# A transformer block with adaptive norms: group 3's V products summed on VectorE instead of TensorE, group 0's second norm in two parts

## The chip, the core and the metric

The kernel runs on one core of a Trainium2 chip. The metric is the device time of one execution in microseconds (us). TensorE is called PE here, VectorE DVE, ScalarE ACT, GpSimd POOL and SyncE, which issues nearly all DMAs, SP, as the profile calls them.

## What is computed

```python
# x: 2048 rows of 512;  sa, ca, ga, sb, cb, gb = six parts of silu(c) @ w_mod
h = layernorm(x) * (1 + ca) + sa
q, k, v = h @ wqkv                                  # 32 heads of 16
logits[h, s, w] = q[h, s] . k[h, s - 2*w] / 4       # w = 0..7; s - 2*w < 0 is masked
attn = softmax(logits over w)
o[h, s] = sum over w of attn[h, s, w] * v[h, s - 2*w]
x = x + ga * (o @ wo)
h = layernorm(x) * (1 + cb) + sb
x = x + gb * ((gelu(h @ w_gate) * (h @ w_up)) @ w_down)    # inner width 1792
```

Attention is a window of eight rows at distance two, so it isn't a matrix product over rows: it is eight elementwise products with shifted K, summed over a head's 16 columns, and eight with shifted V, summed over the shifts.

## The kernel before

The 2048 rows are worked in four groups (0 to 3) of 512. For each group: a first norm; its transposition; 12 products for q, k, v (`qkv`, L621; group 0 in halves, L560); logits; softmax; V products; the product with wo (`x1_mm`, L821) added to x (`x1_ev`, L830); a second norm (`norm`, `ln2`); its transposition (`transp`, `transp_ev`, L475, L481, L513) to h; 14 pairs of products g and u (`ffn_mm`, L851); gelu of g to `gl` and a copy of u to `ub` on ACT (L883, L890); their product `hht` on DVE (L901); and eight half products y with w_down (L863), which DVE adds to x as `ot` (L908) and SP stores.

All engines run from one list, `ORDER`: each number names a thread (one generator per kind of work and group), and takes the next instruction from it. Each engine works its instructions strictly in that order and waits in place. Nothing is planned at run time.

**The V path of a group.** Softmax leaves probabilities `e` with rows of a block of 128 by head: partition 32·g + head for row block g, and eight shifts by 128 rows along the free axis. SP stores `e` to memory and loads it back as `PT`, where the partitions are pairs of shift and head (`pt_dma`, L762, L769). V is stored and loaded back four times, shifted, as `V` (`vload`, L659, L667). DVE multiplies both for each j of four (`pv`, L781, 4096 elements each), PE sums over the shifts by a matrix of ones `M` in tiles of 32 columns (`pv_mm`, L800, eight matmuls for each j), and ACT copies the sums to `oT` (`pv_ev`, L811), the left operand of `x1_mm`.

**Buffers.** PSUM has the pools `mm` (4 banks: qkv, g, u, y), `att` (2) and `lg` (1). `gl` and `ub` have three buffers each; a copy into one waits until DVE has made the `hht` of three pairs before. `pv` and `pq` share four buffers called `prod`.

**Group 0's second norm.** Two of its four row blocks are summed on ACT, two on DVE; then comes one reciprocal root for all four on POOL (L452, a `pow`), then four `xn` on DVE (L461). Sixteen transposes on PE (`BY_PE` names it) put them into two PSUM tiles, from which ACT makes h.

Of the kernel before, what the change touches and what calls it, by code (L numbers as in the profile page):

```python
# [106 lines left out]
def kernel(  # L107
# [395 lines left out]
    def transp_ev(key, dkey, dtag, sc, bi, ev, dep):  # L503
        pe = ev in BY_PE
        for dtp in range(2):
            for dd in range(2):
                dt = 2 * dtp + dd

                def f(dt=dt, dtp=dtp, dd=dd):
                    if pe and dt == 0:  # L510
# [2 lines left out]
                    nc.scalar.activation(out=o, in_=B[key, dtp][:, :, dd, :] if pe else o, func=ACT.Identity,  # L513
                                         scale=sc(dt), bias=bi(dt))
# [474 lines left out]
```

## Time and profile before

| what | us |
|---|---|
| median of 3 runs | 236.57 (236.39 to 236.57) |
| the profiled execution | 236.67 |
| its span, first to last instruction | 234.7 |
| PE busy, share of the span | 230.0, 98% |
| DVE busy | 168.8, 72% |
| ACT busy | 150.3, 64% |

A group row of the profile reads: line, engine, operation, what is written from what, shapes, count | busy us in all, mean ns of one | idle time of the engine just before them, and what ended it. A row of the timeline reads: start, duration, engine, line, operation, operands, count. In the chain of work that ended last, each row is a start, a duration and what ran. A DMA row ends with the median us from issue to landing. The 40 slices are of 5.9 us each; a digit is the busy share in tenths. Matmuls are pipelined, and in the groups one of 512 columns shows some 380 ns; in a row of them each adds 216.

### The profile page before, as it was taken

The numbers are of one execution on the slowest core, as the hardware profiler recorded it, in microseconds if no ns is written. First come the engines' busy times: TensorE is split into PE (matmuls) and PEld (weight loads), VectorE is DVE, ScalarE is ACT, GpSimd is POOL, SyncE is SP. The second block draws the span as 40 slices with busy tenths as digits, with TensorE's granted clock in tenths as the row PEclk, the third lists the DMA queues.
The fourth block names the chain that finished last, engine by engine and source line by source line (L and its number), as shares of the span: only waits on it lengthen the run. The fifth ranks groups of instructions, "written<-read, shape, count | busy, mean of one in ns | idle before, by whom it ended". The sixth has DMA issues, their size and how long they took to land.

```text
span 234.7 us, 3714 instructions
## 1 busy us (share of the span) xinstructions
PE 230.0 (98%) x1408; PEld 110.8 (47%) x1408; DVE 168.8 (72%) x242; ACT 150.3 (64%) x281; POOL 19.7 (8%) x37
## 2 busy tenths in 40 slices
PE   7999999999999999999999999999999999999995
PEld 2788454544544444444443444444444444444443
DVE  4799999999999999999999599968422221222222
ACT  6699998588896566947579732084666703666400
POOL 1412323210200000010000004001000000000000
PEclk9999999999999999999999999999999999999999
DMA  6999696997929518036500790500600011000011
GB/s 218 358 340 299 169 249 231 228 313 258 342 80 300 195 14 307 1 61 170 179 3 1 220 270 14 112 22 0 134 3 1 0 45 47 0 0 0 3 45 45
DMA packets 32441, 30.95 MB, mean 132 GB/s; under 512 B 17064, under 2 KB 28328, under 8 KB 32424
## 3 DMA queue, kind: packets, MB, share of 16 engines
q1 hardware_dynamic: 31888, 30.19, 42.4%
q10 hardware_dynamic: 536, 0.53, 0.6%
q8 instruction: 11, 0.18, 0.3%
q14 instruction: 6, 0.05, 0.1%
HBM read 22.78 MB, written 5.31 MB: 120 GB/s over the span
## 4 chain that ended last, share of the span: by engine, by line
PE 85%; DMA 6%; ACT 6%; SPq 1%; issue 1%; ACTq 0%; DVE 0%
PE g_ps L851 20%; PE u_ps L851 20%; PE y_ps L863 19%; PE qkv_ps L621 10%; DMA wm<-in_w_mod_dram 6%; PE x_ps L821 6%; PE o_ps L800 3%; PE LTp L706 3%; PE y_ps L874 1%; PE qkv_ps L560 1%; ACT h L513 1%; ACT hT L513 1%; ACT kT L639 1%; ACT vT L641 1%; PE hTp L475 1%
## 5 line engine op out<-in xcount | busy, mean ns | idle before, releaser
L851 PE MATMUL g_ps<-h,Wg 128*128 128x512 bf16 x224 | 57.7, 379 | 0.1
L851 PE MATMUL u_ps<-h,Wu 128*128 128x512 bf16 x224 | 57.5, 379 | 0.0
L901 DVE TENSOR_TENSOR hht<-gl,ub 128x512 bf16<-128x512 bf16 x56 | 23.1, 419 | 36.8 <-ACT ub L890 36.8
L883 ACT ACTIVATE gl<-g_ps 128x512 bf16<-128x512 f32 x56 | 33.6, 600 | 24.8 <-PE g_ps L851 22.1
L863 PE MATMUL y_ps<-Wd,hht 128*128 128x512 bf16 x210 | 46.1, 379 | 0.0
L890 ACT CAST ub<-u_ps 128x512 bf16<-128x512 f32 x56 | 32.9, 588 | 17.9 <-PE u_ps L851 17.9
L689 DVE TENSOR_TENSOR pq<-qT,kT 128x4096 bf16<-128x4096 bf16 (+1 forms) x17 | 36.3, 2159 | 0.0
L781 DVE TENSOR_TENSOR pv<-PT,V 128x4096 bf16<-128x4096 bf16 x16 | 36.2, 2287 | 0.0
L851 PEld LDWEIGHTS <-Wg 128*128 128x128 bf16 x224 | 21.6, 98 | 27.3 <-issue 1.9
L851 PEld LDWEIGHTS <-Wu 128*128 128x128 bf16 x224 | 21.7, 98 | 26.8 <-issue 0.8
L621 PE MATMUL qkv_ps<-hT,wqkv 128*128 128x512 bf16 x144 | 32.8, 380 | 0.4 <-ACT hT L513 0.3
L863 PEld LDWEIGHTS <-hht 128*128 128x128 bf16 x210 | 20.5, 98 | 24.9 <-issue 0.4
L621 PEld LDWEIGHTS <-wqkv 128*128 128x128 bf16 x144 | 15.9, 114 | 15.8 <-issue 2.6
L908 DVE TENSOR_TENSOR ot<-y_ps,x 128x512 bf16<-128x512 f32 x15 | 10.2, 684 | 17.6 <-PE y_ps L863 17.6
L452 POOL TENSOR_TENSOR rstd<-rstd,neghalf 128x4 f32<-128x4 f32 (+1 forms) x9 | 10.9, 1211 | 120.4 <-DVE rstd L441 62.7
L811 ACT CAST oT<-o_ps 128x512 bf16<-128x512 f32 x16 | 8.9, 597 | 13.8 <-PE o_ps L800 13.8
L821 PE MATMUL x_ps<-woP,oT 128*128 128x512 bf16 x64 | 15.1, 379 | 0.0
L421 DVE BATCH_NORM_STATS2 st<-x 128x6 f32<-128x512 bf16 x19 | 12.5, 680 | 2.6 <-DMA x<-in_A_x_dram 2.5
L513 ACT ACTIVATE h<-h,modT,scl 128x512 bf16<-128x512 bf16 x12 | 8.8, 806 | 4.8 <-DMA h<-xn 4.8
L560 PE MATMUL qkv_ps<-hT,wqkv 128*128 128x256 bf16 x96 | 11.4, 273 | 0.2
L830 DVE TENSOR_TENSOR x<-x_ps,x 128x512 bf16<-128x512 f32 x16 | 10.9, 686 | 0.6 <-PE x_ps L821 0.5
L560 PEld LDWEIGHTS <-wqkv 128*128 128x128 bf16 x96 | 10.2, 114 | 0.9 <-DMA wqkv<-in_A_wqkv_dram 0.4
(80 smaller groups left out, 193.4 us busy)
## 6 DMA issues: line engine op xcount, KB each, us to landing
V<-vscr SPq DMA_DIRECT2D x16, 526.0 KB, 4.8
vscr<-vT SPq DMA_DIRECT2D x4, 528.0 KB, 3.8
wm<-in_w_mod_dram SPq DMA_DIRECT2D x4, 512.0 KB, 6.9
out_dram<-ot SPq DMA_DIRECT2D x15, 128.0 KB, 1.7
Wg<-in_B_w_gate_dram SPq DMA_DIRECT2D x4, 448.0 KB, 6.0
Wu<-in_B_w_up_dram SPq DMA_DIRECT2D x4, 448.0 KB, 7.1
x<-in_A_x_dram SPq DMA_DIRECT2D x3, 512.0 KB, 5.7
Wd<-in_B_w_down_dram SPq DMA_DIRECT2D x3, 512.0 KB, 6.8
```

What stands on the lines that cost most here:

```text
L421: nc.vector.bn_stats(out=k["st", c4][:], in_=src()[:, c4, :])
L513: nc.scalar.activation(out=o, in_=B[key, dtp][:, :, dd, :] if pe else o, func=ACT.Identity, scale=sc(dt), bias=bi(dt))
L560: nc.tensor.matmul(B["qu", h, blk, u][:, jj, :], lhsT=wqkv[blk][:, dt, 2 * u + jj::4], rhs=B["hT", 0][:, 2 * h:2 * h + 2, dt, :], start=st ...
L621: nc.tensor.matmul(ps[:], lhsT=wqkv[blk][:, dt, j::4], rhs=B["hT", sg][:, :, dt, :], start=(dt == 0), stop=(dt == DT - 1))
L689: nc.vector.tensor_tensor(out=B["pq", sg, j][:, :, c0:c1], in0=_ap(B["qT", sg][:, j, c0:c1], [[0, W], [1, c1 - c0]]), in1=_ap(kT[:, j, sg ...
L781: nc.vector.tensor_tensor(out=t[:], in0=_ap(B["PT", sg][:, 0, :], [[SG, 2], [0, 4], [1, SG]]), in1=_ap(v[:, j, 0, :], [[8, 2], [VR, 4], [1 ...
L821: nc.tensor.matmul(ps[:], lhsT=B["oT", sg][:, j, c4 * P:(c4 + 1) * P], rhs=woP[:, j, :], start=(j == 0), stop=(j == 3))
L851: nc.tensor.matmul(ps[:], lhsT=Wt[:, dt, ft * P:(ft + 1) * P], rhs=B["h2T", sg][:, :, dt, :], start=(dt == 0), stop=(dt == DT - 1))
L863: nc.tensor.matmul(ps[:], lhsT=B["hh", sg, ft][:, c4 * P:(c4 + 1) * P], rhs=B["Wd", ft // 4][:, ft % 4, :], start=(ft == 0), stop=(ft == F ...
L883: nc.scalar.activation(out=gl[:], in_=B["g", sg, ft][:], func=ACT.Gelu_apprx_tanh)
L890: nc.scalar.copy(out=ub[:], in_=B["u", sg, ft][:])
L901: nc.vector.tensor_tensor(out=hh[:], in0=B["gl", sg, ft][:], in1=B["ub", sg, ft][:], op=ALU.mult)
```

## The change

1. *Group 3's V path* (`VS = (3,)`). `e` stays where softmax leaves it; it isn't stored and loaded as `PT`. V is loaded so that its partitions agree with `e` (four loads of 32 partitions, `V3`). DVE multiplies (four times 4096 elements, one for each i of four) and then sums over the eight shifts itself by a `tensor_reduce` to 512 elements in bf16 (`O3`). Since O3 has rows along the free axis by head, and `oT` needs heads' columns on partitions, each quarter goes to memory by four DMAs (rows of 128 bf16) and back by one. PE's 32 matmuls and ACT's four copies for group 3 are gone.
2. *Group 0's V products* are made in two halves of 256 rows, and so are their sums (four times 16 matmuls of 256 columns), the copies, and the second norm (two roots on POOL, for two blocks each). Its transposition goes by two DMA transposes of eight blocks in place of PE, and h is scaled in halves, six on ACT and two on DVE. Its x products use the pool `mm`.
3. *Group 1's `vT`* has its buffer in another pool; `qkv` and `ffn_mm` name all their dependencies; the threads have a new order.

The core of the diff:

```diff
-    29, 29, 29, 2, 29, 29, 3, 29, 1, 45, 0, 1, 17, 18, 29, 29, 29, 17, 37, 37, 39, 39, 2, 2, 39, 39, 39, 4, 39,
+    29, 29, 29, 29, 29, 29, 2, 29, 3, 29, 29, 39, 39, 39, 39, 39, 0, 40, 1, 1, 17, 17, 2, 2, 0, 18, 37, 17, 40,
...
-    BY_PE = ("LN1.1", "LN2.0")
+    BY_PE = ("LN1.1",)
...
+        if sg in VS:
+            for g in range(CPS):
+                def f(g=g):
+                    if g == 0:
+                        B["V3", sg] = T("v4", [P, 4, 4, P + VH], BF16, "V3")
+                    src = bass.AP(vscr[sg].tensor, vscr[sg].offset + g * P, [[4 * n, H], [VR, 16], [1, P + VH]])
+                    nc.sync.dma_start(out=B["V3", sg][H * g:H * g + H].rearrange("p i j s -> p (i j) s"), in_=src)
...
     def pt_dma(sg):
+        if sg in VS:
+            for i in range(4):
+                for g in range(CPS):
+                    def f(i=i, g=g):
+                        d = oscr[sg, i]
+                        nc.sync.dma_start(out=bass.AP(d.tensor, d.offset + g * P, [[SG, H], [H * SG, 4], [1, P]]),
+                                          in_=B["O3", sg][H * g:H * g + H, i])
...
+                    nc.sync.dma_start(out=B["oT", sg][:, i, :], in_=oscr[sg, i][:])
...
     def pv(sg):
+        if sg in VS:
+            for i in range(4):
...
+                    nc.vector.tensor_tensor(out=t[:], in0=_ap(B["e", sg][:], [[0, 4], [P, W], [1, P]]),
+                                            in1=_ap(B["V3", sg][:, i, 0, 2:], [[P + VH, 4], [2, W], [1, P]]), op=ALU.mult)
...
+                        nc.vector.tensor_reduce(out=B["O3", sg][:, i], in_=B["pv", sg, i][:].rearrange("p d w s -> p d s w"),
+                                                axis=AX.X, op=ALU.add)
...
+    def pv_half_mm():
+        for h in range(2):
+            for jp in range(2):
...
+                                nc.tensor.matmul(o_ps[H * i:H * i + H, jj, :], lhsT=M[:], rhs=B["pvh", h, jp][:, jj, t, i, :],
+                                                 start=(jj == 0 and t == 0), stop=(jj == 1 and t == 1), tile_position=(0, H * i))
...
+    def transp_half():
+        for h in range(2):
...
+                nc.sync.dma_start_transpose(out=B["h2T", 0][:, 2 * h:2 * h + 2].rearrange("p c d s -> p (c d) s"),
+                                            in_=B["xn2", 0][:, 2 * h:2 * h + 2, :].rearrange("p c d -> p (c d)"))
```

On DVE, around the end of group 1's second stage and the start of group 2's, the order before was this (xn is group 2's second norm, pv are group 3's last products, ot group 1's results, the last rows group 3's x and the first hht of group 2; `hht` numbered in the text as hht 0, 1, ... of a group):

```order
L461 TENSOR_SCALAR xn<-x,mv,rstd 128x512 x4
L781 TENSOR_TENSOR pv<-PT,V_1851 128x4096 x2
L908 TENSOR_TENSOR ot<-y_ps,x 128x512 x3
L830 TENSOR_TENSOR x<-x_ps,x 128x512
L421 BN_STATS st<-x 128x6
```

And now (O is O3, V_1883 is V3, y_ps of `ot` are group 1's):

```order
L463 TENSOR_SCALAR xn<-x,mv,rstd 128x512 x4
L867 TENSOR_REDUCE O_2078<-pv 128x512
L1035 TENSOR_TENSOR ot<-y_ps,x 128x512
L858 TENSOR_TENSOR pv<-e,V_1883 128x4096
L1035 TENSOR_TENSOR ot<-y_ps,x 128x512 x2
L867 TENSOR_REDUCE O_2078<-pv 128x512
L858 TENSOR_TENSOR pv<-e,V_1883 128x4096
L1028 TENSOR_TENSOR hht<-gl,ub 128x512
L867 TENSOR_REDUCE O_2078<-pv 128x512
L858 TENSOR_TENSOR pv<-e,V_1883 128x4096
L1028 TENSOR_TENSOR hht<-gl,ub 128x512 x2
L867 TENSOR_REDUCE O_2078<-pv 128x512
L1035 TENSOR_TENSOR ot<-y_ps,x 128x512
L1028 TENSOR_TENSOR hht<-gl,ub 128x512 x5
```

The four reductions and three products stand ahead of, and between, the first three hht of group 2, and the last ot of group 1 stands behind the fourth reduction. On PE the x products of group 3 moved from behind group 1's last y and the first g of group 2 to behind g 9 of group 2.

On SP's queue the same stretch before held stores and two transposes:

```order
L932 DMA out_dram<-ot 128x512
L481 DMA_TRANSPOSE h_2096<-xn 128x16x128
L932 DMA out_dram<-ot 128x512
L481 DMA_TRANSPOSE h_2226<-xn 128x16x128
L932 DMA out_dram<-ot 128x512 x9
```

Now the sums' stores and loads stand between them:

```order
L483 DMA_TRANSPOSE h_2042<-xn 128x16x128
L1059 DMA out_dram<-ot 128x512
L791 DMA oscr_0_116<-O_2078 32x4x128 x3
L1059 DMA out_dram<-ot 128x512
L791 DMA oscr_0_116<-O_2078 32x4x128
L798 DMA oT<-oscr_0_116 128x512
L791 DMA oscr_1_117<-O_2078 32x4x128 x4
L798 DMA oT<-oscr_1_117 128x512
L791 DMA oscr_2_118<-O_2078 32x4x128 x4
L798 DMA oT<-oscr_2_118 128x512
L791 DMA oscr_3_119<-O_2078 32x4x128 x4
L798 DMA oT<-oscr_3_119 128x512
```

Each quarter of `oT` is loaded behind its four stores; two out stores and group 3's transpose wait behind the last.

Around group 0's second norm DVE had this order before (x is group 0's sum; mx and LTp belong to group 1's softmax):

```order
L830 TENSOR_TENSOR x<-x_ps,x 128x512 x2
L723 TENSOR_REDUCE mx<-LTp 128x128
L830 TENSOR_TENSOR x<-x_ps,x 128x512 x2
L421 BN_STATS st<-x 128x6 x2
L427 BN_AGGR mv<-st 128x2 x2
L441 TENSOR_SCALAR rstd<-mv 128x2
L446 TENSOR_SCALAR rstd<-sums 128x2
L729 TENSOR_TENSOR LTp<-LTp,mx 128x1024
L461 TENSOR_SCALAR xn<-x,sums,rstd 128x512 x2
L461 TENSOR_SCALAR xn<-x,mv,rstd 128x512 x2
```

Now its second half stands so:

```order
L929 TENSOR_TENSOR x<-x_ps,x 128x512 x2
L463 TENSOR_SCALAR xn<-x,sums,rstd 128x512
L423 BN_STATS st<-x 128x6
L463 TENSOR_SCALAR xn<-x,mv,rstd 128x512
L429 BN_AGGR mv<-st 128x2
L443 TENSOR_SCALAR rstd<-mv 128x1
L448 TENSOR_SCALAR rstd<-sums 128x1
L744 TENSOR_REDUCE mx<-LTp 128x128
L463 TENSOR_SCALAR xn<-x,sums,rstd 128x512
L463 TENSOR_SCALAR xn<-x,mv,rstd 128x512
L750 TENSOR_TENSOR LTp<-LTp,mx 128x1024
L710 TENSOR_TENSOR pq<-qT,kT 128x4096
```

The first half's statistic and roots now stand ahead of the last two x sums, and a product of group 2's logits stands between the last xn and the two half h that DVE makes (L956, not shown).

More of the change, by code (lines that the diff above doesn't have):

```diff
@@ L147 @@
     gscr = {b: dram.tile([D], BF16, name=f"gscr{b}") for b in (2, 3, 4, 5)}
+    oscr = {(g, i): dram.tile([P, SG], BF16, name=f"oscr{g}_{i}") for g in (3,) for i in range(4)}
     escr = [dram.tile([P, W, P], BF16, name=f"escr{g}") for g in range(NSG)]
@@ L624, in qkv @@
             tk = [SL["q"]] if (blk, j) == (0, 0) else []
-            yield Op("PE", 0.865, f, after=[f"LN1.{sg}.h{d}" for d in (2, 3)] + [wq0(blk, d) for d in range(DT)], take=[SL["mm"]] + tk,
+            yield Op("PE", 0.865, f, after=[f"LN1.{sg}.h{d}" for d in range(DT)] + [wq0(blk, d) for d in range(DT)], take=[SL["mm"]] + tk,
                      give=[SL["hT"]] if last else [], fire=f"qp.{sg}.{blk}.{j}")
@@ L650, in f @@
                 nc.gpsimd.memset(B["vT", 0][:, :, 0:VH], 0.0)
-        yield Op("POOL", 0.2, f, after=[f"vh.{sg - 1}"] if sg else [], take=[SL["vs"]], fire=f"vz.{sg}")
+        yield Op("POOL", 0.2, f, after=[f"vh.{sg - 1}"] if sg else [], take=[SL["ot4" if sg == 1 else "vs"]], fire=f"vz.{sg}")
     def vload(sg):
@@ L760, in pt_dma, with f @@
     def pt_dma(sg):
+        if sg in VS:
[5 more added lines that the diff above has]
+                                          in_=B["O3", sg][H * g:H * g + H, i])
+                    yield Op("SP", 0.4, f, after=[f"pr.{sg}.{i}"], give=[SL["hT"]] if i == 3 and g == 3 else [], fire=f"os.{sg}.{i}.{g}", lat=0.6)
+                def f(i=i):
+                    if i == 0:
+                        B["oT", sg] = T("ot4", [P, 4, SG], BF16, "oT")
+                    nc.sync.dma_start(out=B["oT", sg][:, i, :], in_=oscr[sg, i][:])
+                yield Op("SP", 0.4, f, after=[f"os.{sg}.{i}.{g}" for g in range(CPS)], take=[SL["ot4"]] if i == 0 else [], fire=f"oT.{sg}.{i}", lat=0.6)
+            return
         def f():
@@ L773, with pv_half, f @@
     smp = {k: pool(k + "_p", 1) for k in ("mx", "e", "ssum", "rinv", "PT")}
-    def pv(sg):
+    def pv_half():
+        for h in range(2):
+            for j in range(4):
+                def f(h=h, j=j):
+                    if j % 2 == 0:
+                        B["pvh", h, j // 2] = T("prod", [P, 2, 2, 4, 256], BF16, "pv")
+                    nc.vector.tensor_tensor(out=B["pvh", h, j // 2][:, j % 2],
+                                            in0=_ap(B["PT", 0][:, 0, 256 * h:], [[SG, 2], [0, 4], [1, 256]]),
+                                            in1=_ap(B["V4", 0][:, j, 0, 256 * h:], [[8, 2], [VR, 4], [1, 256]]), op=ALU.mult)
+                last = h == 1 and j == 3
+                yield Op("DVE", 1.15, f, after=["pt.0.1", f"V4.0.{j}"], take=[SL["prod"]] if j % 2 == 0 else [],
+                         give=[SL["v4"], SL["PT"]] if last else [], fire="pv.0.3" if last else f"pvh.{h}.{j}")
@@ new lines, in pv_half_mm, with f @@
+    def pv_half_mm():
+        for h in range(2):
+            for jp in range(2):
+                def f(h=h, jp=jp):
+                    o_ps = T("att", [P, 2, 256], F32, "o_ps")
+                    B["oh", h, jp] = o_ps
+                    for jj in range(2):
+                        for t in range(2):
+                            for i in range(4):
+                                nc.tensor.matmul(o_ps[H * i:H * i + H, jj, :], lhsT=M[:], rhs=B["pvh", h, jp][:, jj, t, i, :],
+                                                 start=(jj == 0 and t == 0), stop=(jj == 1 and t == 1), tile_position=(0, H * i))
+                yield Op("PE", 0.44, f, quad=True, after=["pv.0.3" if h and jp else f"pvh.{h}.{2 * jp + 1}", "consts"],
+                         take=[SL["att"]], give=[SL["prod"]], fire=f"oh.{h}.{jp}")
@@ new lines, in pv_half_ev, with f @@
+    def pv_half_ev():
+        for h in range(2):
+            for jp in range(2):
+                def f(h=h, jp=jp):
+                    if ("oT", 0) not in B:
+                        B["oT", 0] = T("ot4", [P, 4, SG], BF16, "oT")
+                    nc.scalar.copy(out=B["oT", 0][:, 2 * jp:2 * jp + 2, 256 * h:256 * h + 256], in_=B["oh", h, jp][:])
+                yield Op("ACT", 0.485, f, after=[f"oh.{h}.{jp}"], take=[] if h or jp else [SL["ot4"]], give=[SL["att"]],
+                         fire=f"oTh.{h}.{jp}")
@@ new lines, in pv, with f @@
+    def pv(sg):
+        if sg in VS:
+            for i in range(4):
+                def f(i=i):
+                    t = T("prod", [P, 4, W, P], BF16, "pv")
+                    B["pv", sg, i] = t
+                    nc.vector.tensor_tensor(out=t[:], in0=_ap(B["e", sg][:], [[0, 4], [P, W], [1, P]]),
+                                            in1=_ap(B["V3", sg][:, i, 0, 2:], [[P + VH, 4], [2, W], [1, P]]), op=ALU.mult)
+                yield Op("DVE", 2.2, f, after=[f"p.{sg}"] + [f"V4.{sg}.{g}" for g in range(CPS)], take=[SL["prod"]],
+                         give=[SL["v4"], SL["es"]] if i == 3 else [], fire=f"pv.{sg}.{i}")
+                def f(i=i):
+                    if i == 0:
+                        B["O3", sg] = T("hT", [P, 4, 4, P], BF16, "O3")
+                    with nc.allow_low_precision("the eight terms add up in f32; only the sum is rounded, as it is on its way from PSUM"):
+                        nc.vector.tensor_reduce(out=B["O3", sg][:, i], in_=B["pv", sg, i][:].rearrange("p d w s -> p d s w"),
+                                                axis=AX.X, op=ALU.add)
+                yield Op("DVE", 4.4, f, take=[SL["hT"]] if i == 0 else [], give=[SL["prod"]], fire=f"pr.{sg}.{i}")
+            return
@@ L822, in f @@
                                      start=(j == 0), stop=(j == 3))
-            yield Op("PE", 0.865, f, after=[f"oT.{sg}.3", "woS"], take=[SL["att"]], give=[SL["ot4"]] if c4 == 3 else [],
+            yield Op("PE", 0.865, f, after=([f"oTh.{c4 // 2}.{jp}" for jp in range(2)] if sg == 0 else [f"oT.{sg}.{i}" for i in ((0, 1, 2, 3) if sg in VS else (3,))]) + ["woS"], take=[SL["att" if sg else "mm"]], give=[SL["ot4"]] if c4 == 3 else [],
                      fire=f"x1p.{sg}.{c4}")
@@ new lines, in transp_half, with f @@
+    def transp_half():
+        for h in range(2):
+            def f(h=h):
+                if h == 0:
+                    B["h2T", 0] = T("h2", [P, CPS, DT, P], BF16, "h2")
+                nc.sync.dma_start_transpose(out=B["h2T", 0][:, 2 * h:2 * h + 2].rearrange("p c d s -> p (c d) s"),
+                                            in_=B["xn2", 0][:, 2 * h:2 * h + 2, :].rearrange("p c d -> p (c d)"))
+            yield Op("SP", 0.9, f, after=[f"LN2.0.x{2 * h + 1}"], take=[] if h else [SL["h2"]], give=[SL["xn"]] if h else [],
+                     fire=f"LN2.0.th{h}", lat=0.6)
@@ new lines, with half_ev, f @@
+    HALF_DVE = ((1, 2), (1, 3))
+    def half_ev(eng):
+        for h in range(2):
+            for dt in range(DT):
+                if ((h, dt) in HALF_DVE) != eng:
+                    continue
+                def f(h=h, dt=dt):
+                    o = B["h2T", 0][:, 2 * h:2 * h + 2, dt, :]
+                    if eng:
+                        nc.vector.tensor_scalar(out=o, in0=o, scalar1=scl[:, 4 + dt:5 + dt], scalar2=modT[:, 4 + dt:5 + dt],
+                                                op0=ALU.mult, op1=ALU.add)
+                    else:
+                        nc.scalar.activation(out=o, in_=o, func=ACT.Identity, scale=scl[:, 4 + dt:5 + dt],
+                                             bias=modT[:, 4 + dt:5 + dt])
+                yield Op("DVE" if eng else "ACT", 0.25 if eng else 0.5, f, after=[f"LN2.0.th{h}", "mod3", "mod4"],
+                         fire=f"LN2.0.h{dt}.{h}")
@@ L956 @@
     pl.spawn(exp_table())
+    for sg in range(1, NSG):
+        pl.spawn(ln1_ev(sg, True))
+    for sg in range(NSG):
+        pl.spawn(ln2_ev(sg, True) if sg else half_ev(True))
+    pl.spawn(ln2(0, 2, 4))
+    pl.spawn(norm_act(lambda: B["x", 0], lambda c4: [f"x1.0.{c4}"], "LN2.0", 2))
     with tc.manual_schedule():
```

58 lines of the change are left out of this document (37 added, 21 removed), and 71 rows, old and new, of the table ORDER.

## The prediction

> **What bounds the kernel now.** I read the page's engine shares and slices first, then the waits of the matmul engine, then the chain in order of time.
>
> ```profile
> span 234.7 us, 3714 instructions
> PE 230.0 (98%) x1408; PEld 110.8 (47%) x1408; DVE 168.8 (72%) x242; ACT 150.3 (64%) x281; POOL 19.7 (8%) x37
> ...
> PE   7999999999999999999999999999999999999995
> ...
> DVE  4799999999999999999999599968422221222222
> ```
>
> TensorE (PE) is busy in 38 of 40 slices to nine tenths or more, so it is the bound from one end to the other. VectorE (DVE) is as full until slice 27 (about 160 us) and nearly idle after it. Work that leaves PE is therefore worth its time, and work that arrives on DVE is free only where DVE's answers still come before PE asks for them.
>
> ```profile
> PE warm_ps L204 <- DVE gB L199: 1.2, 1, 1.2
> PE qkv_ps L621 <- ACT hT L513: 0.3, 1, 0.3
> PE gR_ps L370 <- DMA wm<-in_w_mod_dram: 0.2, 1, 0.2
> ```
>
> PE's whole list of waits is 1.7 us: there is almost no waiting left to remove, so a gain can come only from PE work taken out, and a loss only from a new wait. The chain shows the places that the change touches:
>
> ```profile
> 19.09 1.00 PE hTp L475 x16
> ...
> 57.84 5.18 PE qkv_ps L621 x24
> 64.38 2.14 ACT h L513 x3
> ...
> 141.84 10.58 PE y_ps L863 x49
> 152.41 1.84 PE o_ps L800 x32
> 154.25 1.62 PE y_ps L863 x7
> ...
> 160.35 0.86 PE u_ps L851 x4
> ...
> 183.66 12.09 PE y_ps L863 x56
> ```
>
> The 32 products of group 3's V path stand inside group 1's last products and cost 1.84 us. One product of the second stage (four matmuls, g or u) costs 0.86, a group's eight down products 12.09, a set of sixteen transposes on PE 1.00.
>
> **What the change costs, part by part.**
>
> *Group 3's V products.* PE loses the 32 o_ps matmuls: −1.84. The copies of o_ps on ScalarE go too; ScalarE waited there anyway, so I count nothing for them. DVE keeps four products of 4096 elements and gets four reductions from 4096 to 512 elements, bf16 in SBUF. The trace has no such reduction; these rows bound it:
>
> ```profile
> L781 DVE TENSOR_TENSOR pv<-PT,V 128x4096 bf16<-128x4096 bf16 x16 | 36.2, 2287 | 0.0
> ...
> L901 DVE TENSOR_TENSOR hht<-gl,ub 128x512 bf16<-128x512 bf16 x56 | 23.1, 419 | 36.8 <-ACT ub L890 36.8
> ...
> L421 DVE BATCH_NORM_STATS2 st<-x 128x6 f32<-128x512 bf16 x19 | 12.5, 680 | 2.6 <-DMA x<-in_A_x_dram 2.5
> ...
> L908 DVE TENSOR_TENSOR ot<-y_ps,x 128x512 bf16<-128x512 f32 x15 | 10.2, 684 | 17.6 <-PE y_ps L863 17.6
> ...
> L723 DVE TENSOR_REDUCE mx<-LTp 128x128 f32<-128x1024 f32 x4 | 4.9, 1218 | 0.0
> ...
> L689 DVE TENSOR_TENSOR pq<-qT,kT 128x2048 bf16<-128x2048 bf16 x2 | 2.4, 1212 | 0.0
> ```
>
> The bf16 product takes 1212 ns for 2048 elements and 2287 for 4096, so 1075 per 2048 and 137 fixed. A reduction of 1024 f32 elements takes 1218, so 1081 per 1024 behind the same 137: half the product's rate. The low end for the new reduction is the product's 2.29 us, the high end 4 × 1081 + 137 = 4.46 us. I take the high end: it is the same operation, and the one row that folds bf16 from SBUF, the statistics over 512 elements, takes 680 ns, as long as a sum with an f32 operand in PSUM (684) and not the 419 of a bf16 product.
>
> The Trainium skill ("VectorE: DVE Perf Modes", section on the perf-mode tier table) says that tensor_reduce has a program for one element per cycle alone, in bf16 as in f32, in SBUF as in PSUM. It agrees with the f32 row's 1218 ns; no run here shows it for bf16. By that rule the sum is the one below; by the rate of the bf16 product row it would be the 234.6 of the first rival.
>
> Now the place. What counts is what stands behind the reductions on DVE. These rows set the clock of that stretch:
>
> ```profile
> 138.03 1.28 DVE L830 TENSOR_TENSOR x<-x_ps,x 128x512 bf16<-128x512 f32 x2
> ...
> 143.79 2.98 POOL L452 TENSOR_TENSOR rstd<-rstd,neghalf 128x4 f32<-128x4 f32 x1 [42.55 <-DVE rstd L441]
> ...
> 146.81 1.38 DVE L461 TENSOR_SCALAR xn<-x,mv,rstd 128x512 bf16<-128x512 bf16 x4 [0.30 <-POOL rstd L452]
> 148.10 4.49 DVE L781 TENSOR_TENSOR pv<-PT,V 128x4096 bf16<-128x4096 bf16 x2
> ...
> 162.84 1.11 POOL L452 TENSOR_TENSOR rstd<-rstd,neghalf 128x4 f32<-128x4 f32 x1 [16.07 <-DVE rstd L441]
> ```
>
> Two products in a row take 4.49 where one takes 2.29: the next instruction starts 0.08 before the last ends. So the steps are 2.20 for a product, 4.38 for a reduction, 0.60 for an ot or a statistic, 0.34 for an hht. I count from Y, the start of group 1's down products (141.84 before). The x sums end at 139.31, Y − 2.5. Then on DVE: two statistics and an aggregate 1.3, the first product 2.2, aggregates 0.3, three hht 1.0: Y + 2.3. The reciprocal root on GpSimd takes 1.11, or 2.98 beside a product; here only short hht stand beside it, so the four xn start near Y + 3.2 and end at Y + 4.6. From there the order is fixed: reduction 9.0, ot 9.6, product 11.8, two ot 13.0, reduction 17.4, product 19.6, **hht 0 of group 2 at 19.9**, reduction 24.3, product 26.5, **hht 1 and 2 at 26.8 and 27.2**, reduction 31.5, **last ot of group 1 at 32.1**.
>
> PE: group 2's products begin at Y + 12.1, one each 0.864 us. There are three buffers each of gl and ub between ScalarE and DVE, so the copy of g 3 waits for hht 0, that of g 4 for hht 1. Of the four PSUM banks for products group 1's last y keeps one until that last ot; with three left, u 4 takes g 3's bank and u 5 takes g 4's. So u 4 (due at 19.9) waits for a copy behind hht 0 and starts at 20.6; u 5 (due 21.6, with that delay 22.3) waits for a copy behind hht 1, 26.8 + 0.1 + 0.6 = 27.5; u 7, due at 12.1 + 15 × 0.864 = 25.05, takes the bank of the last ot and starts at 32.2. Sum of the new waits: **+7.1 us**. Nothing hides it: PE's queue holds only these products there, and the x products of group 3 stand behind g 9.
>
> *The sums' way by DMA.* Sixteen stores of 32 KB in rows of 256 bytes and four loads of 128 KB stand on SP's queue; behind them wait two out stores and the last transpose, which have time. What counts is the last:
>
> ```profile
> 106.95 0.33 SPq L762 DMA_DIRECT2D escr<-e  x1
> ```
>
> ```profile
> V<-vscr SPq DMA_DIRECT2D x16, 526.0 KB, 4.8
> ...
> out_dram<-ot SPq DMA_DIRECT2D x15, 128.0 KB, 1.7
> ...
> Wu<-in_B_w_up_dram SPq DMA_DIRECT2D x4, 448.0 KB, 7.1
> ...
> PT<-escr SPq DMA_DIRECT2D x8, 128.0 KB, 2.3
> ...
> h<-xn SPq DMA_TRANSPOSE x3, 4.4
> hT<-xn SPq DMA_TRANSPOSE x2, 6.4
> ```
>
> The last reduction ends at Y + 31.6. Four issues of 0.33, the fourth store landed after 1.7 as an out store, then a load of 2.3 as PT: Y + 36.6. The delayed PE starts group 3's first x product at 32.2 + 4 × 0.864 = 35.7 and needs the last part 0.65 later, at 36.3. With both transfers at V's 4.8 the wait would be 5.9, at best 0; the stores' short rows make them somewhat slower than an out store, and I take **+1.0**. Group 3's V loads and its probabilities leave earlier than they are needed (V for the first product at Y − 1.2) and cost nothing.
>
> *Group 0's second norm.* PE loses sixteen transposes, −1.00, which go to two DMA transposes of eight blocks. Behind the last x product PE had eight qkv products (the first six are the chain's 5.18), the transposes and a gate product, 8.2 us; now it has eight qkv products and one block of logits, 8 × 0.864 + 0.6 = 7.5. The chain beside it: x sum 0.69, statistic, xn and aggregates 1.5, root on GpSimd, two xn, the transfer, two half h on ScalarE:
>
> ```profile
> L452 POOL TENSOR_TENSOR rstd<-rstd,neghalf 128x2 f32<-128x2 f32 x2 | 1.5, 752 | 4.5 <-DVE rstd L441 4.1 <-DVE rstd L446 0.4
> ...
> L531 ACT ACTIVATE hT<-hTp,modT,scl 128x256 bf16<-128x256 bf16 x3 | 1.6, 560 | 1.2 <-PE hTp L498 1.2
> ```
>
> 0.69 + 1.5 + 0.75 + 0.7 + 1.1 = 4.8 beside the transfer. That is between 2.2 (half of h's 4.4) and hT's 6.4; landing has a part that does not shrink, so I take 3.5. 8.3 against 7.5: **+0.8**, between 0 and 3.7. Together −0.2. SP's queue holds the two transposes ahead of the last quarter of Wu, group 1's V and wm5. The quarter leaves some 0.9 behind the second transpose and u 0 needs it 3.5 + 1.1 − 0.9 + 1.5 = 5.2 later; at Wu's 7.1 it would be 1.9 late, at an out store's 1.7 in time. I take 0, since the queues are no longer full of the loads among which 7.1 was measured.
>
> *The rest.* Group 0's V products in halves are the same elements on DVE and the same columns on PE, with four more fixed 0.14 on DVE: hidden while DVE's next answer is a logit for which PE has qkv products. The gate products wm3 to wm5 move and cost the same elsewhere. At the start ScalarE's chain is a kT copy shorter ahead of group 2's hT; that lets PE reach the second norm earlier and wait there longer. I count 0, ± 0.7.
>
> **Sum.** The profiled execution took 236.67 us (its span 234.7 and 2.0 around it; the three runs' median is 0.10 lower). 236.67 − 1.84 − 0.2 + 7.1 + 1.0 = **242.7 us**.
>
> **Rivals.**
> - *The reduction runs as fast as a bf16 product* (step 2.20). Then hht 1 is done at 4.6 + 3 × 2.2 + 3 × 2.2 + 3 × 0.6 + 2 × 0.34 = 20.3, its copy at 21.0, before the 21.6 at which u 5 is due; the last ot at 23.4, before 25.05; the sums land at 28.0, before the x product's due 29.1. No wait: 236.67 − 1.84 − 0.2 = 234.6, faster by 0.9%. The wait grows by four times the step, 4p − 10.35; it eats the 2.04 of gain at a step of 3.1 us, which is where the sign turns. For it: DVE does take bf16 at double rate in products. Against it: the two rows of folding instructions.
> - *The sums' transfers are slow*: 4.8 each in place of 1.7 and 2.3: 242.7 + 4.9 = 247.6. For it: rows of 256 bytes; against it: the queues are nearly empty there.
> - *The second norm's transfer is late* by hT's 6.4: 242.7 + 2.9 = 245.6; with the fast reduction 237.5, which is slower as well. For it: weight loads share the queues at that time.
> - *The change takes nothing from PE's path*: the matmuls go, but other waits fill exactly the place, and the time stays at 236.5. It needs a step near 3.1.
>
> **How the numbers follow.** The main case has 0.79, the slow transfers and the late norm 0.06 together, the fast reduction 0.12, the even case 0.03. Within the main case the unknowns are −1.0 and +4.9 of the sums' way, −0.8 and +2.9 of the norm, ± 0.7 at the start, and some tenths of the root: these alone rarely add up, so its own range is 239.8 to 246; to hold 8 in 10 over all cases I give 239.0 to 246.5. A difference under 0.2% can't be told from none here. Slower: 0.79 + 0.06, less a hundredth = 0.84; within 0.2%: 0.03; faster: 0.13, the fast reduction and an early start.
>
> **What would show it.** The group of TENSOR_REDUCE with O as output: mean near 4460 ns (right) or near 2290 (the first rival). PE's waits: u_ps on ScalarE's gl with one piece near 5 us, and on DVE's ot near 1; x_ps on a DMA of oT near 1; g_ps on h after group 0's norm under 2. PE's slices dip once, at about 165 us. PE's busy time falls by near 2.8. If DVE's hht 1 of group 2 comes less than 22 us after Y, the forecast is wrong.

## The result: 254.75 us, slower by 7.9%

The changed kernel's median is 254.75 us (254.55 to 256.44, four runs), against 236.48 for the kernel before on the same chip: a ratio of 1.0788 (1.0741 to 1.0835). The forecast was 242.7, with 246.5 as its upper end. The direction was right; the loss, 18.3 us, was three times as large as forecast, and outside the range. The ratios here and below leave out two executions that the record counts as slow: one of the kernel before (240.10) and one of e_hh_first (258.57).

The page of the changed kernel (profiled execution 254.94 us):

```profile
span 253.2 us, 3709 instructions
PE 232.0 (92%) x1381; PEld 110.2 (44%) x1392; DVE 196.9 (78%) x254; ACT 148.4 (59%) x279; POOL 18.5 (7%) x38
...
PE   8999989999799999999999998843679999999995
...
DVE  4699998999999999999996989999977532222222
...
PEclk9999999999999999999999999997599999999999
```

PE has one new deep hole, in slices 25 to 30, and a shallow one in slice 11 (the wait at group 0's second norm, below). DVE, which had been nearly idle after slice 27, is full in the deep one. TensorE's busy time has not fallen by the forecast's 2.8 us: it has risen by 2.0, though 16 matmuls fewer are issued (the weight loads fell from 1408 to 1392; the trace lacks some matmul records), because the granted clock dips inside the hole. The same stretch by engines (column by column: stretch, its length, busy time of PE, PEld, DVE, ACT and POOL, then the granted clock, the DMA share and GB/s):

```profile
156.00:190.00 34.00, 20.75 (x77) 8.10 (x76) 32.60 (x18) 9.53 (x18) 0.00 (x0) 0.85 0.14 35
```

In those 34 us DVE works 32.60 and PE 20.75: DVE sets the pace and PE waits for it. PE's and ScalarE's waits say for what, and the chain says which instruction of DVE's it was:

```profile
PE u_ps L978 <- ACT gl L1010: 10.0, 2, 6.2
PE u_ps L978 <- DVE ot L1035: 3.2, 2, 1.8
PE g_ps L978 <- ACT h L959: 1.6, 1, 1.6
```

```profile
ACT gl L1010 <- DVE hht L1028: 19.0, 4, 8.4
```

```profile
148.69 7.05 DVE O L867
155.74 0.60 DVE ot L1035
...
159.73 7.04 DVE O L867
166.78 2.20 DVE pv L858
168.97 0.34 DVE hht L1028
169.31 6.96 DVE O L867
176.27 2.20 DVE pv L858
...
179.14 7.01 DVE O L867
186.15 0.61 DVE ot L1035
...
186.80 1.02 PE u_ps L978 x4
```

It is the queue that the prediction described, instruction for instruction: PE's u products wait for ScalarE's copy to gl, that copy waits for an hht of group 2, and the hht stands behind a reduction to O; the last of the waits ends at group 1's last ot, behind the fourth reduction. What differs is one number, the reduction itself:

```profile
L867 DVE TENSOR_REDUCE O<-pv 128x512 bf16<-128x4096 bf16 x4 | 28.4, 7108 | 0.0
```

7.11 us each, where the forecast had taken 4.46 as the upper end.

**Where the 18.3 us are.** Group 1's down products began at 143.90 in the changed kernel and 141.46 before (starts of the first weight load in the trace): 2.4 us were lost ahead of that point. Of these, 1.9 lie between group 0's last x product and that point, at group 0's second norm and behind it: 86.09 us, before 84.21 (the last weight load of the x products starts at 57.81, before at 57.25). The other 0.6 came earlier and belong to this execution: e_tree below, which has the changed kernel's instructions up to that point, was at 56.81 and 142.90, again 86.09 us apart but 1.0 earlier. From the start of group 1's down products to the start of the last product it took 103.02 us, before 87.15: 15.9 more, of which the forecast's gain of about 2 is already taken off.

### The profile page after: what moved, and what is told of

It reads as the page before. It is cut to its first block, busy times and chain, and to the rows that moved or that the text cites. A ratio compares the mean times of both kernels' runs of the same rounds, so it can differ in the third digit from the quotient of the medians.

```text
span 253.2 us, 3709 instructions
## 1 busy us (share of the span) xinstructions
PE 232.0 (92%) x1381; PEld 110.2 (44%) x1392; DVE 196.9 (78%) x254; ACT 148.4 (59%) x279; POOL 18.5 (7%) x38
## 4 chain that ended last, share of the span: by engine, by line
PE 63%; DVE 18%; ACT 13%; DMA 2%; issue 1%; POOL 1%; ACTq 0%; DVEq 0%
PE u_ps L978 16%; PE g_ps L978 16%; PE y_ps L990 13%; DVE O L867 11%; PE qkv_ps L632 7%; PE x_ps L920 4%; DVE pv L858 3%; DMA wm<-in_w_mod_dram 2%; ACT hT L524 2%; PE LTp L727 2%; ACT gl L412 2%; PE o_ps L897 2%; ACT gl L406 1%; ACT h L959 1%; PE y_ps L1001 1%
## 5 line engine op out<-in xcount | busy, mean ns | idle before, releaser
L978 PE MATMUL u_ps<-h,Wu 128*128 128x512 bf16 x224 | 59.4, 389 | 13.2 <-ACT gl L1010 10.0
L978 PE MATMUL g_ps<-h,Wg 128*128 128x512 bf16 x224 | 59.4, 388 | 1.7 <-ACT h L959 1.6
L978 PEld LDWEIGHTS <-Wu 128*128 128x128 bf16 x224 | 22.0, 100 | 42.5 <-issue 18.4
L867 DVE TENSOR_REDUCE O<-pv 128x512 bf16<-128x4096 bf16 x4 | 28.4, 7108 | 0.0
L632 PEld LDWEIGHTS <-wqkv 128*128 128x128 bf16 x144 | 15.9, 114 | 16.9 <-issue 3.8
L454 POOL TENSOR_TENSOR rstd<-rstd,neghalf 128x4 f32<-128x4 f32 (+1 forms) x10 | 9.8, 975 | 152.4 <-DVE rstd L443 95.6
L524 ACT ACTIVATE h<-h,modT,scl 128x512 bf16<-128x512 bf16 x12 | 8.8, 802 | 18.4 <-DMA h<-xn 18.4
L876 DVE TENSOR_TENSOR pv<-PT,V 128x4096 bf16<-128x4096 bf16 x8 | 18.1, 2286 | 0.2 <-PE LTp L727 0.2
```

The costliest lines, as they stand in the source:

```text
L632: nc.tensor.matmul(ps[:], lhsT=wqkv[blk][:, dt, j::4], rhs=B["hT", sg][:, :, dt, :], start=(dt == 0), stop=(dt == DT - 1))
L867: nc.vector.tensor_reduce(out=B["O3", sg][:, i], in_=B["pv", sg, i][:].rearrange("p d w s -> p d s w"), axis=AX.X, op=ALU.add)
L876: nc.vector.tensor_tensor(out=t[:], in0=_ap(B["PT", sg][:, 0, :], [[SG, 2], [0, 4], [1, SG]]), in1=_ap(v[:, j, 0, :], [[8, 2], [VR, 4], [1 ...
L978: nc.tensor.matmul(ps[:], lhsT=Wt[:, dt, ft * P:(ft + 1) * P], rhs=B["h2T", sg][:, :, dt, :], start=(dt == 0), stop=(dt == DT - 1))
```

## The experiments

Each compares with the kernel before on the same chip. "The tree" below is the name for the three additions that replace the reduction.

### m_reduce: what a reduction costs on VectorE

A kernel of its own, with a list of sums over eight terms, three times each. The lines differ in type, in place and in how far apart the eight terms lie (`v(t, k)` views t so that they lie k elements apart):

```
tensor_reduce(out=o(ob, 128), in_=v(src, 128))       # L41, bf16, 256 bytes apart, as in the changed kernel
tensor_reduce(out=ob, in_=src as (s w))              # L43, bf16, side by side
tensor_reduce(out=o(ob, 4), in_=v(src, 4))           # L45, bf16, 8 bytes apart
tensor_reduce(out=o(ob, 8), in_=v(src, 8))           # L46, bf16, 16 bytes apart
...
tensor_reduce(out=of, in_=srcf as (w s), 1024)       # L52, f32 in SBUF, 512 bytes apart
tensor_reduce(out=o(of, 128), in_=v(srcf, 128))      # L53, f32 in SBUF, 512 bytes apart
tensor_reduce(out=of, in_=psf as (w s), 1024)        # L54, f32 in PSUM, 512 bytes apart
tensor_reduce(out=of, in_=srcf as (s w))             # L55, f32 in SBUF, side by side
```

> This kernel leaves the whole computation out and writes a constant; it only runs sums over eight terms on VectorE, each kind three times, to find why the changed kernel's reduction of 128x4096 took 7.11 us (1.70 ns an element) where the forecast had 4.46 (1081 ns for 1024 elements, 1.06 ns an element). Every line reads 4096 elements unless said otherwise; the eight terms lie k elements apart. Theory A, the distance of the terms in SBUF sets the price: line 43 (bf16, terms side by side) near 4.4 us, rising by lines 44 to 49 (2, 4, 8, 16, 32, 64 apart) to 7.1 at line 41 (128 apart) and at 50 (512 apart); f32 at 128 apart (line 53) no faster than 7.1 and f32 side by side (line 55) near 4.4. Theory B, bf16 sets the price: line 43 also near 7.1, line 53 (f32) near 4.4, line 52 (1024 f32) near 1.1 and line 51 (1024 bf16) near 1.8. Theory C, a cost for each of the 512 sums: all of 41 to 55 with 4096 elements near 7.1 and those with 1024 near 1.8, except line 54 (1024 f32 from PSUM, as in the kernel's maximum), near 1.1. Lines 56 to 58 are the same sum as three bf16 additions (2048, 1024, 512): near 1.13, 0.60 and 0.34 us, 2.07 together, if they go at the 2.29 us for 4096 of the bf16 products.

```profile
L46 DVE TENSOR_REDUCE ob<-srcb 128x512 bf16<-128x4096 bf16 x3 | 21.6, 7184 | 0.0
L53 DVE TENSOR_REDUCE of<-srcf 128x512 f32<-128x4096 f32 x3 | 21.1, 7023 | 0.0
...
L41 DVE TENSOR_REDUCE ob<-srcb 128x512 bf16<-128x4096 bf16 x3 | 20.9, 6958 | 0.0
L55 DVE TENSOR_REDUCE of<-srcf 128x512 f32<-128x4096 f32 x3 | 13.2, 4413 | 0.0
...
L45 DVE TENSOR_REDUCE ob<-srcb 128x512 bf16<-128x4096 bf16 x3 | 13.2, 4412 | 0.0
L43 DVE TENSOR_REDUCE ob<-srcb 128x512 bf16<-128x4096 bf16 x3 | 13.2, 4411 | 0.0
L52 DVE TENSOR_REDUCE of<-srcf 128x128 f32<-128x1024 f32 x3 | 5.6, 1863 | 0.0
...
L54 DVE TENSOR_REDUCE of<-psf 128x128 f32<-128x1024 f32 x3 | 3.7, 1217 | 0.0
```

Theory A, the distance, holds; the type does not matter (L53 against L41, L55 against L43), and a cost for each of the 512 sums is out, since L43 makes as many as L41. It is a step and not a slope, though: 4.41 us up to 8 bytes, 7.0 to 7.5 from 16 bytes on. And the last two rows are the pair that the forecast lacked: 1024 f32 elements with the terms 512 bytes apart take 1.22 us when they lie in PSUM and 1.86 when they lie in SBUF. The row `mx<-LTp` of the profile, from which the forecast took its price, reads PSUM. The tree's additions were 1.22, 0.69 and 0.42 us here (2048, 1024 and 512 elements). Each stood beside an instruction that did not need its result, and the next one started 0.09 before its end: 2.1 together.

### m_reduce2: bytes or elements, and do other instructions pay

> This kernel leaves the whole computation out and writes a constant; each line runs three times on VectorE. The first such kernel gave 4.41 us for 4096 elements whose eight terms lie 8 bytes apart or less, 7.0 to 7.5 from 16 bytes on, and from PSUM 1.22 us for 1024 at 512 bytes apart, where SBUF took 1.86. Theory, the distance in bytes in SBUF sets the price: line 45 (f32, 8 bytes) near 4.4, line 46 (f32, 16 bytes) near 7.0, line 47 (4032 elements of bf16, 12 bytes) between or at one of them, and a maximum (line 48) as slow as a sum, 7.0; from PSUM lines 49 and 50 (side by side; 64 bytes apart) both near 1.2; lines 51 (512 elements) and 52 (2048) near 1.0 and 3.5 by 1.70 ns an element. Rival, the number of terms skipped sets it and not the bytes: line 45 near 4.4, 46 near 4.4. Lines 53 to 57 ask whether a copy and a product of 4096 bf16 lose time as well when they read with the terms 256 bytes apart (53) or write 16 bytes apart (54, 56), against 55 and 57 in order (57 near 2.29): theory, they do, 4.3 to 7; rival, only a reduction does, and all are near 2.3 or below.

```profile
L56 DVE TENSOR_TENSOR qb<-srcb 128x4096 bf16<-128x4096 bf16 x3 | 54.9, 18286 | 0.0
L54 DVE COPY qb<-srcb 128x4096 bf16<-128x4096 bf16 x3 | 27.7, 9231 | 0.0
L46 DVE TENSOR_REDUCE of<-srcf 128x512 f32<-128x4096 f32 x3 | 22.1, 7370 | 0.0
...
L47 DVE TENSOR_REDUCE ob<-srcb 128x504 bf16<-128x4032 bf16 x3 | 16.5, 5515 | 0.0
...
L45 DVE TENSOR_REDUCE of<-srcf 128x512 f32<-128x4096 f32 x3 | 13.2, 4399 | 0.0
...
L57 DVE TENSOR_TENSOR qb<-srcb 128x4096 bf16<-128x4096 bf16 x3 | 6.9, 2294 | 0.0
...
L50 DVE TENSOR_REDUCE of<-psf 128x128 f32<-128x1024 f32 x3 | 3.7, 1222 | 0.0
```

Bytes decide: f32 at 8 bytes (L45) is fast, at 16 bytes (L46) slow, and bf16 at 12 bytes (L47) lies between. From PSUM 64 bytes apart (L50) cost nothing. A maximum is as slow as a sum (L48, 6.98 us), and a copy that reads 256 bytes apart takes 4.56 us instead of 1.23 (L53 against L55), both as expected. The expectation for writes was too low: a product that writes its bf16 results 16 bytes apart takes 18.29 us instead of 2.29 (L56 against L57), a copy 9.23 (L54). Letting the products write the eight terms side by side would save the reduction some 2.6 us (7.0 to 4.4) and cost the product 16, by an estimate from these rows; it was not tried in the kernel.

### e_five: the forecast's price for the reduction

```
-  in_=B["pv", sg, i][:].rearrange("p d w s -> p d s w")
+  in_=B["pv", sg, i][:, :, 0:5].rearrange("p d w s -> p d s w")
```

> The changed kernel, but the reduction sums five of the eight shifts (three are left out), so that its step takes what the forecast had priced: 5/8 of 7.03 us is 4.4 us. Theory: the forecast's relation, TensorE's wait = 4p - 10.35, holds and only p was wrong; with p = 4.4 the wait is 7.2 us and the time 236.67 - 1.84 + 7.2 + 2.4 (what after lost ahead of group 1's down products) = 244.4 us, 243.4 to 245.6. Rival: the loss belongs to the place (what stands behind the reductions and the way of the sums through DRAM), not to the reduction's length; then most of the 15.9 us lost behind that point stays, and the time is above 249.

Measured: 244.29 us (244.19 to 245.33), ratio 1.0327 (1.0299 to 1.0354), as the theory said to a tenth, but by two errors that cancel: 1.3 us and not 2.4 were lost ahead of group 1's down products (142.73 against 141.46), and 6.3 and not 5.4 behind that point (93.45 against 87.15). The reductions took 4.52 us, and the long wait is the forecast's: a piece of 5.1, for which it had said "near 5". Its wait of about 1 for group 1's last ot did not appear (last section).

```profile
L867 DVE TENSOR_REDUCE O<-pv 128x512 bf16<-128x2560 bf16 x4 | 18.1, 4520 | 0.0
```

```profile
PE u_ps L978 <- ACT gl L1010: 5.8, 2, 5.1
```

### e_tree: the same place, a sum of 2.3 us

```
-  nc.vector.tensor_reduce(out=B["O3", sg][:, i], in_=..., axis=AX.X, op=ALU.add)
+  t = B["pv", sg, i]
+  nc.vector.tensor_tensor(out=t[:, :, 0:4], in0=t[:, :, 0:4], in1=t[:, :, 4:8], op=ALU.add)
+  nc.vector.tensor_tensor(out=t[:, :, 0:2], in0=t[:, :, 0:2], in1=t[:, :, 2:4], op=ALU.add)
+  nc.vector.tensor_tensor(out=B["O3", sg][:, i], in0=t[:, :, 0], in1=t[:, :, 1], op=ALU.add)
```

> The changed kernel in its own order, with the reduction replaced by three bf16 additions in place (2048, 1024 and 512 elements), so that a step takes about 2.07 us instead of 7.03. Theory: 4p - 10.35 is below zero, so no wait is left in group 2's g and u products: 236.67 - 1.84 + 2.4 = 237.2 us, 236.5 to 238.3. Rival, the place and the transfers cost by themselves: 245 or more.

Measured: 236.57 us (235.94 to 238.99), ratio 1.0003 (0.9979 to 1.0026). A step takes 2.32 us (the first starts at 147.60, the next instruction behind its third addition at 149.93) and not the expected 2.07: here each addition needs the result of the one before it and starts 0.03 behind its end. Not one wait for gl or ot is left in PE's list; what remains of the changed kernel's new waits is the 1.6 us for h at group 0's first g product.

```profile
L867 DVE TENSOR_TENSOR pv<-pv 128x2048 bf16<-128x2048 bf16 x4 | 4.9, 1218 | 0.0
L868 DVE TENSOR_TENSOR pv<-pv 128x1024 bf16<-128x1024 bf16 x4 | 2.8, 692 | 0.1
L869 DVE TENSOR_TENSOR O<-pv 128x512 bf16<-128x512 bf16 x4 | 1.7, 425 | 0.1
```

Three kernels with one order and three steps p of a sum test the forecast's relation. The stretch is that from the start of group 1's down products to the start of the last product:

| kernel | step p, us | stretch, us | over the tree's | 4p − 10.35 |
|---|---|---|---|---|
| before | – | 87.15 | – | – |
| e_tree | 2.32 | 85.04 | – | below 0 |
| e_five | 4.44 | 93.45 | 8.4 | 7.4 |
| changed | 7.01 | 103.02 | 18.0 | 17.7 |

The tree's stretch is 2.1 us shorter than before's: this is the gain that the change was worth without its waits. Where e_five's 1.0 beyond the relation went is in the last section.

### e_hh_first: the long reductions in an order meant to hold nothing back

Only the order differs from the changed kernel; group 3's x products move into group 2's down products. On DVE:

```
- O, ot, pv, ot, ot, O, pv, hht 0, O, pv, hht 1, hht 2, O, ot, hht 3 ...
+ O, ot, pv, ot, ot, ot, O, hht 0 to 3, pv, hht 4, O, hht 5 to 8, pv, hht 9, O, hht 10 to 13
```

> The changed kernel with its reductions of 7.11 us, but with nothing held behind them that was there already: all of group 1's scaled outputs stand ahead of the second reduction, group 2's hh products 0 to 3 ahead of the third product, 5 to 8 ahead of the fourth, and group 3's output product and second norm are moved into group 2's down products, where the sums now come. Theory: the queue is only half of it; 28.4 us of reductions among 9 us of products also put group 3's sums at about 191 us and its last scaled norm near 209, 14 us behind before, of which TensorE has work for some; 250 us, 247 to 253. Rival, only the place of the reductions cost: 236.67 - 1.84 + 2.4 + about 2 for the first u products = 239, 237 to 241.

Measured: 256.83 us (253.71 to 258.57), ratio 1.0813 (1.0764 to 1.0863). The rival's 237 to 241 is far off: this order does not save the 7-us reduction. The theory's own figure was 7 too low as well, and which of its terms was short is not known. Nor are the old waits all gone: PE still waits 4.6 us for gl and 2.4 for ot. The trace is of the fastest run, 253.71; its chain:

```profile
172.32 7.03 DVE O L868
...
183.85 7.03 DVE O L868
...
193.91 2.02 DMA oT<-oscr
195.97 1.25 PE x_ps L921 x5
...
205.39 4.27 DMA h<-xn
...
210.40 2.22 ACT h L525 x3
```

The last sum is done at 190.9, group 3's h at 212.6, and PE, out of other work, waits for it. So the two ends of the problem are one in both orders tried: whatever stands behind the reductions is late, be it group 2's hht or group 3's norm. DVE works 45.8 of the 51 us from 144 to 195. That no order at all could hide 28 us of reductions is argued from this and not shown.

### e_g3tree: group 3's part alone, with the tree

Group 0 as before; group 3's products with the tree (+ on DVE, behind group 2's last xn, against the changed kernel's order); before's order up to group 2's x products.

```
- BY_PE = ("LN1.1",)
+ BY_PE = ("LN1.1", "LN2.0")
- ("pv", lambda q: pv(q) if q else pv_half()), ...
+ ("pv", pv), ("pvmm", pv_mm), ("pvev", pv_ev), ...
- O, ot, pv, ot, ot, O, pv, hht 0, O, pv, hht 1, hht 2, O, ot, hht 3 ...
+ sum, ot, pv, ot, ot, sum, pv, ot, hht 0, sum, pv, hht 1 to 3, sum, hht 4 ...
```

> Group 0 as in the kernel before (its norm by TensorE transposes, its V products whole), and group 3's V products as in the changed kernel with the three additions for the reduction; the order is that of before up to the first product of group 3's V and that of after behind it, with group 1's last scaled output and group 2's first hh products ahead of the third sum. Theory: group 3's part now only takes its 1.84 us of matmuls from TensorE, and the 2.4 us lost ahead of group 1's down products belong to group 0's part and the order there: 236.67 - 1.84 = 234.8 us, 234.2 to 235.6, faster than both kernels. Rival: the loss ahead of group 1's down products is not group 0's: 237.2.

Measured: 234.74 us (234.31 to 235.20), ratio 0.9915 (0.9893 to 0.9936), 2.0 us faster than before; the theory's 234.8. A second time:

> The kernel with group 0 as before and group 3's products summed by three additions once more, on whatever chip and start this call gets: 234.7 us again, 234.3 to 235.4. Rival, that its first lead was the scatter of its start: 235.6 to 236.6.

Measured: 234.56 us (234.36 to 234.70), ratio 0.9912 (0.9897 to 0.9928). This version beats both kernels. Between it and e_tree lie 1.8 us by the medians (1.5 by the two traces up to group 1's down products, 142.90 against 141.43). That is group 0's part with the order that goes with it, and part 3 of the change, which this kernel takes back as well.

### e_g0only: group 0's part alone

The changed kernel's order up to group 0's first hht, before's behind it.

```
- VS = (3,)
+ VS = ()
```

> Group 0's part alone: V products and second norm of group 0 in two parts, with DMA transposes, in the changed kernel's order up to group 0's first hh product; group 3 as before, and before's order from there on. Theory: the changed norm puts the first u product of group 0 at 68.48 instead of 66.57 us and nothing behind it gives that back, so 236.57 + 1.9 = 238.5 us, 238.0 to 239.1. Rival, as the forecast had it (-0.2, the added wait is paid for by the transposes taken from TensorE): 236.4, 236.0 to 236.8.

Measured: 241.38 us (241.07 to 242.40), ratio 1.0212 (1.0191 to 1.0232), more than either had said. The first u product came at 68.34, the theory's 1.8 late (0.4 of it at group 0's last x product already); but before's order behind it does not fit, and group 1's o_ps matmuls now wait for its products:

```profile
PE o_ps L897 <- DVE pv L876: 2.1, 2, 1.8
```

So this run shows that the part costs and does not price it; the difference of e_tree and e_g3tree bounds it better.

### e_late_exp and e_halves_v: what of group 0's part costs

The first moves only ScalarE's exp of group 1 behind group 0's last h (the order on ScalarE):

```
- h 0, 1, 2 of the first half, exp, h 3 of the first half, h 0, 1 of the second
+ h 0, 1, 2, 3 of the first half, h 0, 1 of the second, exp
```

> The kernel with three additions in the changed kernel's order (236.57 us in its own runs), with one thing moved: ScalarE's exp of group 1 stands behind group 0's last scaled transpose, not between the third and the fourth; the sum and reciprocal that need it move with it. Theory: the exp's 1.0 us stood on the path to group 0's first g product, whose wait for h (1.6 us) falls to about 0.6, so 235.6 us, 235.1 to 236.1. Rival: VectorE's two scaled halves (done at 66.75 us behind a 2.28-us product of group 2) or the second transfer end last in any case, or group 1's softmax then comes late: no change, 236.3 to 236.9.

Measured: 236.79 us (235.82 to 239.05), ratio 1.0006 (0.9968 to 1.0044): the rival's no change. PE's wait for h fell from 1.6 to 0.7, as expected, and a wait of 0.6 for ScalarE's copy of kT came in its place. Twelve runs that scatter by 3 us could hardly tell the theory's 1.0; the traces can: from group 0's last x product to its first down product it is 41.9 us in e_tree and here (56.81 to 98.67, 57.23 to 99.17). The second takes TensorE's transposes back and leaves the V products in halves:

```
- BY_PE = ("LN1.1",)
+ BY_PE = ("LN1.1", "LN2.0")
- ("t2", lambda q: transp(...) if q else transp_half()), ("h2", lambda q: ln2_ev(q) if q else half_ev(False))
+ ("t2", lambda q: transp(...)), ("h2", ln2_ev)
```

> The kernel with three additions in the changed kernel's order, with group 0's V products in halves as there, but its second norm as before: one rstd of four blocks, TensorE's transposes, ScalarE's four scaled copies of 512. Theory, the transposes by DMA cost most of the 1.8 us between the kernel with three additions (236.57) and the one with group 0 as before (234.74): TensorE's wait of 1.6 us for h at the first g product falls below 0.7, and with the transposes' 1.0 us back on TensorE and the norm's last block about 1 us later on VectorE it is 235.7 us, 235.1 to 236.2. Rival, the order on VectorE ahead of the norm costs it (a 2.2-us product of group 1 and group 1's maximum stand among the norm's steps): 236.6, 236.3 to 237.4.

Measured: 236.95 us (236.32 to 238.57), ratio 0.9996 (0.9967 to 1.0026): again the rival's. PE's wait for h fell to 0.6, as the theory had it, but with the transposes back on PE the first u product stands 10.7 us behind the last x product, as in e_tree; ahead of its exp ScalarE waited 0.8 for DVE's difference of group 1. The two chains through the place, of the changed kernel and of the one with the late exp:

```profile
63.43 0.52 ACT qT L648
...
64.00 1.59 ACT h L959 x3
65.59 0.91 ACT LTp L755
66.50 1.51 ACT h L959 x3
...
68.05 0.81 PE g_ps L978 x3
```

```profile
63.42 3.11 ACT h L961 x6
66.53 0.91 ACT LTp L756
67.44 0.52 ACT kT L651
```

In both, ScalarE works from 63.4 us without a gap through h, exp and the copies of q and k that free PSUM; PE waits for the one or for the other. What stands there is the same list in another sequence. Before, the exp ran from 61.8 to 62.8, ahead of it; now group 1's maximum and difference come later on DVE and the exp falls into the middle. That this list as a whole, and no single member, makes the 1.8 us fits all three runs; it was not shown by a kernel that shortens it, and stays open to that extent.

## Why the prediction was right in direction and wrong in size

- **The matmuls taken from PE, −1.84: about right.** The tree's stretch is 2.1 shorter, e_g3tree as a whole 2.0.
- **The reduction, 4.46 us as the high end: wrong, and the step that failed.** It measured 7.11. The rows offered as bounds were no bounds: the 1218 ns belonged to operands in PSUM, and no row of the profile read bf16 from SBUF with 256 bytes between the terms. The prediction named type and operation as what might differ; it was the place, with a distance that is dear in SBUF and free in PSUM (m_reduce). The rule that it weighed, from the Trainium skill's "VectorE: DVE Perf Modes" (section on the perf-mode tier table), one element per cycle in any type and place, holds for terms side by side (4.41 us for 4096, 1.08 ns each) and does not speak of distance. Another page of the Trainium skill, "Vector Engine (DVE) Microarchitecture Reference" (section "Measured stream behaviour on trn2"), does, and the forecast had not weighed it: in a program of two sources of 32-bit words it has 1.73 ns a column where one source hops 4 KiB at every element. Carried over to one bf16 source that hops 256 bytes, this is an estimate of 4096 × 1.73 = 7.1 us. The trace agrees, with 7.11.
- **The wait, 4p − 10.35: right.** With the measured step of 7.01 it gives 17.7, and 18.0 was measured; with e_five's 4.44 it gives 7.4 against 8.4. Of the way from the forecast's 7.1 to the measured 18.0, four times the error of one step is 10.5. The list of DVE's work holds to some tenths: with a step of 7.01 it puts the end of group 1's last ot 42.6 us behind the start of the down products, and it was 42.8 (186.74). The point at which the sign turns, p = 3.1, stands between e_tree and e_five.
- **The sums' way by DMA, +1.0: the way right, the wait not there.** In e_g3tree the last stores are issued from 165.67 on, the load at 168.65, and it landed 2.0 later, 5.0 us in all as forecast; PE's weight load waited 0.3 for it. In the changed kernel the last load, issued at 189.16, landed at 191.17, about when the first x product (190.62) came to its last part; PE's list has no wait for it. The 1.0 held a margin that was not needed.
- **Group 0's norm, −0.2: wrong by about 2.** Behind the last x product 1.9 us were lost up to group 1's down products, in the changed kernel and in e_tree alike. The transfers (3.1 and 3.0 us, 3.5 taken) were not the fault. The transposes' 1.0 bought only 0.4 between the last x product (first weight load at 57.17, before 56.60) and the first g product, and the wait for h was 1.6 instead of 0.8. The sum priced the chain x, root, transfer, h as if ScalarE were free when the transfer landed; it is the engine with the longest list there, and still in exp (to 66.49) when the second transfer had landed (65.98).
- **PE's busy time, −2.8: wrong, +2.0.** In e_tree, where the long waits are gone, it is 226.8, 3.2 below before; the changed kernel's 5.2 above that are matmuls that ran slower behind the waits (below).
- **The range** took 4.46 as a wall. With 7.1 admitted as an upper end the same relation gives 253.4 (236.67 − 1.84 − 0.2 + 17.8 + 1.0). That this is within 1.4 of the measured time is in part luck: group 0's −0.2 was too low by about 2 and the +1.0 for the sums' way too high by 1.

## What to carry to other kernels

A price for a new instruction is safe only from a row that agrees in operation, type, memory and distance between neighbours. Here the row's terms were 512 bytes apart too, but in PSUM, and it was no bound for terms in SBUF; the type made no difference. So look at what a wide step between elements does on that engine. Sum a few planes by additions over whole planes rather than by a reduction across them: 2.3 us against 7.0 here, for the same eight terms. And write the wait as a function of the unknown step, as was done here: one measured number then explains 10.5 of the 12.0 us by which the forecast missed.
